# Moving six transposes of x from TensorE to DMA, cutting later loads into 3 KB runs, and starting attention work earlier in the second pass

## The chip, the cores and the metric

The kernel runs on one core of a Trainium2 chip. A core has five engines with instruction streams of their own: TensorE (PE, matrix products, with its weight loads shown apart as PEld), VectorE (DVE), ScalarE (ACT), GpSimd (POOL) and SyncE (SP), and sixteen DMA engines that move data between the memories. The time of a run is the device time of the one core in microseconds (us); lower is better. The time before the change is the median of three runs, 248.25 us (248.21 to 249.76).

## The reference

The reference computes an attention whose keys and values are mixed between blocks, and feeds its output to a gated feed-forward network. Cut to what matters:

```python
B, H, S, D = 4, 8, 768, 64              # batches, heads, tokens, head size; 8 blocks of C = 96 tokens
P = sort_net                            # (B, H, 8, 8)
for _ in range(5):                      # exp, divide by row sums, divide by column sums
    P = exp(P - P.max(-1)); P /= P.sum(-1); P /= P.sum(-2)
k_sorted = einsum('bhij,bhjcd->bhicd', P, k_blocks)    # the same for v
attn = softmax(q_block @ k_sorted_block.T / sqrt(D))   # within each block of 96 tokens
x = (attn @ v_sorted_block) -> (B * S, H * D)          # 3072 tokens x 512
g, val = x @ w_gate, x @ w_val          # 512 -> 1536
out = (g * sigmoid(g) * val) @ w_out    # 1536 -> 512, float32
```

Inputs and output are float32. The kernel multiplies in bf16 and accumulates in float32.

## The kernel before, in words

**Tiles and stages.** The feed-forward part works in eight passes, `ffn(0)` to `ffn(7)`; pass n takes 384 tokens: half of batch n // 2. A pass has 12 steps m. `gate(n, m)` and `value(n, m)` are four matmuls each, of 128 x 384, over the four chunks kc of the model dimension; ACT takes a tanh of the gate's result and two DVE operations make the product h. In between stand the output products of the pass before, `outp(n - 1, t3, part)`: three row tiles of 128 tokens, each in three parts of four matmuls of 128 x 512. ACT copies a finished tile to SBUF and SP writes it out.

**Attention.** x for a pass comes from four units of attention, unit u = half * 4 + g, and unit g of a half makes exactly chunk kc = g of the pass's x. So `gate(n, 0)` needs unit 0's (or 4's) part first and unit 3's (or 7's) part as its fourth matmul. A unit is: `scores` (8 matmuls of the stored keys against queries into a PSUM tile of two banks, tagged "a" or "b"), `exps` on ACT, `av` (8 matmuls into a tile of the same tag, then on DVE a reciprocal and a product that writes the tile `st`, from a pool of three). `st` has tokens on partitions; the feed-forward part wants them along the free dimension. Two ways lead there. `xtr` makes four PE transposes into PSUM (`x_to`, L352) and a DVE copy into the tile `xt`. `x_dma` (L367) issues one transposing DMA from SP's queue, `st` to `xt`, and PE and DVE do nothing.

**Which unit takes which way.** `units()` (L542) decides: batch 0 and the first four units of batch 1 by PE, all later ones by DMA. The first four units of batch 0 are written out by hand ahead of the passes (L497 to L528).

**Order of the work.** PE's and POOL's order is the order of the program text (a manual schedule); DVE's, ACT's and SP's order is left to the framework's scheduler after L538. `merge(main, side)` (L570) lays the side work into a pass: main items have costs in us (0.65 for a gate or value, 0.87 for a part of an output product), and a side item is put in after the first main item with which the sum of costs reaches its due time. In pass 1 the side work is: `kq_chunk` for batch 1, three times two chunks of 16 (keys mixed and queries turned, 64 matmuls in all for each due time, one chunk drained by DVE and one by ACT), `v_chunk` for batch 1 (four times 16 matmuls), and then units 0 to 3 of batch 1. Within `units`, a pair of units has its scores at `at`, the second exp at `at + 1.3`, the two `av` at `at + 1.9` and `at + 3.6`, and each PE transpose a `lag` after its `av`.

**Loads.** All loads that convert float32 to bf16 are issued by POOL, in order, and travel on the software queue q0; SP's transfers travel on the hardware queue q1. POOL issues batch 0's v, q and k, the weights, batch 1's v (L157), k and q (L159 to L161, in two pieces of 64 and 32 tokens of each block), the output weights, and then behind four copies of v, keys and values of batches 2 and 3 (`load_k_pair`, L599, L600) and the conversion of their queries into a scratch tensor in DRAM (`q_cast`, L370). A load's tile is one row of 96 x 64 elements for each partition, so that a whole row of k or v lands as one run of 12,288 bytes.

**The end.** The last row tile's output (`out_halves`, L430) is made in two halves of 256 columns; ACT drains the first, DVE the second, and SP writes each out.

## Time and profile before

| of the profiled execution | value |
|---|---|
| its own device time | 248.79 us |
| its span, from the first to the last instruction | 246.7 us |
| PE busy | 236.6 us (96% of the span) |
| PE weight loads busy | 140.3 us (57%) |
| DVE busy | 157.7 us (64%) |
| ACT busy | 109.8 us (45%) |
| POOL busy | 50.3 us (20%) |
| granted TensorE clock | 1.00 |
| bytes on q0 (POOL's loads) | 14.16 MB in 18480 packets |
| bytes on q1 (SP's transfers) | 9.84 MB in 18176 packets |

The span is shorter than the device time by 2.1 us, which lie around it. The profiled execution is 0.54 us above the median of the three runs. In the answers of the trace a line gives the start in us, the time that the instructions take together, engine, line, operation, output and inputs, shape, count, and in brackets how long the engine sat idle before it and which work ended that. A matmul's shown time is longer than its share of a stream, because matmuls overlap: the cost of one in a stream is the distance from its start to the next one's.

Pass 0 begins at about 25 us, pass 1 at 43.1 us and pass 2 at 77.0 us.

### The profile page before, as it was taken

To read this page: it belongs to the slowest core of one execution; us is meant where nothing else is said; L and a number is where in the kernel's file an instruction comes from. 1 tells how busy PE (TensorE), PEld (TensorE's weight loads), DVE (VectorE), ACT (ScalarE), POOL (GpSimd) and SP (SyncE) were. 2 spreads that over 40 slices of the span, in tenths; PEclk is the share of its full clock that TensorE was granted. 3 is DMA by queue.
4 is the path that set the end of the run, shared out by engine and by line. 5 is a ranking of instruction groups with operands and counts; after the bars stand their busy time and mean duration, and the time that the engine had idled before them with its cause. 6 is when DMAs were issued, how large, how long until landed. Compare 5 with 4: busy or idle time off the path is not lost.

```text
span 246.7 us, 6160 instructions
## 1 busy us (share of the span) xinstructions
PE 236.6 (96%) x2609; PEld 140.3 (57%) x2633; DVE 157.7 (64%) x332; ACT 109.8 (45%) x186; POOL 50.3 (20%) x44
## 2 busy tenths in 40 slices
PE   6799999998999999999999999999999999999995
PEld 6375666575555566655555655565555555555543
DVE  6786779888455685867557746755764585446700
ACT  3977653364444444354642642254245334222311
POOL 5992139990098000000000000000000000000000
PEclk9999999999999999999999999999999999999999
DMA  5989999999999195110121111112111211100122
GB/s 96 215 121 208 206 220 210 203 224 222 183 183 161 40 201 127 45 45 0 45 74 35 58 58 35 44 43 78 32 43 45 50 48 53 43 27 20 43 82 88
DMA packets 36682, 24.38 MB, mean 99 GB/s; under 512 B 27696, under 2 KB 32560, under 8 KB 36272
## 3 DMA queue, kind: packets, MB, share of 16 engines
q0 software_dynamic: 18480, 14.16, 37.6%
q1 hardware_dynamic: 18176, 9.84, 14.2%
q8 instruction: 20, 0.33, 0.5%
q14 instruction: 6, 0.05, 0.1%
HBM read 28.32 MB, written 7.86 MB: 147 GB/s over the span
## 4 chain that ended last, share of the span: by engine, by line
PE 84%; DVE 7%; issue 3%; ACT 2%; DMA 2%; DVEq 0%; POOLq 0%
PE g_ps L386 24%; PE v_ps L404 24%; PE o_ps L421 23%; PE tkq L245 3%; PE qk L308 3%; PE av_ps L335 3%; DMA v<-in_v_dram 2%; DVE st L341 2%; DVE vt L223 1%; DVE gs_sb L396 1%; PE o_ps L437 1%; DVE h L409 1%; PE idle_ps L447 1%; PE tv L276 1%; PE x_ps L352 1%
## 5 line engine op out<-in xcount | busy, mean ns | idle before, releaser
L396 DVE SCALAR_TENSOR_TENSOR gs_sb<-th_sb,g_ps 128x384 bf16<-128x384 bf16 x96 | 52.9, 551 | 46.6 <-ACT th_sb L394 43.5
L404 PE MATMUL v_ps<-xt,wv_sb 128*128 128x384 bf16 x380 | 77.3, 326 | 0.1
L386 PE MATMUL g_ps<-xt,wg_sb 128*128 128x384 bf16 x376 | 76.6, 325 | 0.2
L394 ACT ACTIVATE th_sb<-g_ps 128x384 bf16<-128x384 f32 x96 | 47.2, 491 | 57.7 <-PE g_ps L386 55.1
L421 PE MATMUL o_ps<-wo,h 128*128 128x512 bf16 x255 | 62.1, 379 | 1.3 <-issue 0.3
L409 DVE SCALAR_TENSOR_TENSOR h<-v_ps,gs_sb 128x384 bf16<-128x384 f32 x96 | 53.3, 556 | 7.1
L404 PEld LDWEIGHTS <-wv_sb 128*128 128x128 bf16 x380 | 35.4, 97 | 23.9 <-issue 1.0
L386 PEld LDWEIGHTS <-wg_sb 128*128 128x128 bf16 x376 | 35.0, 97 | 24.3 <-issue 0.6
L421 PEld LDWEIGHTS <-h 128*128 128x128 bf16 x276 | 25.8, 98 | 27.9
L426 ACT COPY o_sb<-o_ps 128x512 f32<-128x512 f32 x23 | 13.5, 586 | 45.2 <-PE o_ps L421 45.2
L124 POOL COPY vch<-v 64x1536 bf16<-64x1536 bf16 (+2 forms) x11 | 28.7, 2639 | 14.1 <-DMA v<-in_v_dram 14.0
L321 ACT ACTIVATE e_all<-qk 96x768 bf16<-96x768 f32 x30 | 22.5, 802 | 8.4 <-PE qk L308 8.4
L341 DVE TENSOR_TENSOR st<-av_ps,r_sb 96x512 bf16<-96x512 f32 x32 | 21.7, 680 | 0.2
L335 PEld LDWEIGHTS <-e_all 96*128 96x128 bf16 x256 | 11.9, 98 | 4.9 <-ACT e_all L321 0.9
L339 DVE RECIPROCAL r_sb<-av_ps 96x8 f32<-96x8 f32 x32 | 6.4, 199 | 12.3 <-PE av_ps L335 12.2
L335 PE MATMUL av_ps<-vt,e_all 96*128 96x65 bf16 x256 | 13.1, 193 | 0.1
L223 DVE CAST vt<-tv 96x1024 bf16<-96x1024 f32 (+1 forms) x9 | 9.8, 1098 | 2.6 <-PE tv L286 1.7
L225 ACT CAST vt<-tv 96x1024 bf16<-96x1024 f32 (+1 forms) x9 | 8.1, 914 | 5.5 <-PE tv L286 3.6
L447 PE MATMUL idle_ps<-warm_sb 128*128 128x512 bf16 x22 | 6.1, 381 | 0.4 <-issue 0.2
L223 DVE COPY oh_sb<-o_ps 128x256 f32<-128x256 f32 x1 | 0.4, 425 | 9.3 <-PE o_ps L437 9.3
L371 POOL DMA_DIRECT2D q_scr<-in_q_dram x2 | 5.7, 3232 | 0.0
L122 ACT COPY vch<-v 64x768 bf16<-64x768 bf16 (+1 forms) x4 | 5.5, 1387 | 0.3 <-DMA v<-in_v_dram 0.3
(80 smaller groups left out, 133.1 us busy)
## 6 DMA issues: line engine op xcount, KB each, us to landing
out_dram<-o_sb SPq DMA_DIRECT2D x23, 256.0 KB, 2.0
v<-in_v_dram POOLq DMA_DIRECT2D x4, 384.0 KB, 12.7
wg_sb<-in_moe_w_gate_dram POOLq DMA_DIRECT2D x3, 512.0 KB, 11.3
wv_sb<-in_moe_w_val_dram POOLq DMA_DIRECT2D x3, 512.0 KB, 13.1
wo<-in_moe_w_out_dram POOLq DMA_DIRECT2D x3, 512.0 KB, 15.8
kp<-in_k_dram POOLq DMA_DIRECT2D x2, 768.0 KB, 10.0
v<-in_v_dram POOLq DMA_DIRECT2D x2, 768.0 KB, 16.5
q_scr<-in_q_dram POOLq DMA_DIRECT2D x2, 768.0 KB, 25.0
```

The source lines that it names most:

```text
L124: eng.tensor_copy(dst, src.transpose([0, 2, 1]))
L223: nc.vector.tensor_copy(dst, src)
L321: nc.scalar.activation(e_all[:, n:n + 2, 0:4 * C], wide[0:C, :, 0:4 * C], AF.Exp, scale=scale)
L335: nc.tensor.matmul(o[:, two, i4, 0:D + 1], lhsT=e[:, i4 * C:i4 * C + 128], rhs=vt[:, 2 * g + two, half * 4 + i4, 0:D + 1], start=True, sto ...
L341: nc.vector.tensor_tensor(st.rearrange("p i two d -> p two i d"), o[0:C, :, :, 0:D], r_sb.to_broadcast([C, 2, 4, D]), op=ALU.mult)
L386: nc.tensor.matmul(g_ps, lhsT=wg_sb[:, kc, ts(m, 128)], rhs=xt[:, kc, :], start=(kc == 0), stop=(kc == NKC - 1))
L394: nc.scalar.activation(th_sb, g_ps, AF.Tanh, scale=0.5)
L396: nc.vector.scalar_tensor_tensor(gs_sb, th_sb, 1.0, g_ps, op0=ALU.add, op1=ALU.mult)
L404: nc.tensor.matmul(v_ps, lhsT=wv_sb[:, kc, ts(m, 128)], rhs=xt[:, kc, :], start=(kc == 0), stop=(kc == NKC - 1))
L409: nc.vector.scalar_tensor_tensor(h_tiles[n][:, m, :], v_ps, 0.5, gs_tiles.pop(m), op0=ALU.mult, op1=ALU.mult)
L421: nc.tensor.matmul(o_ps, lhsT=h_w[:, m, ts(t3, 128)], rhs=wo_sb[part][:, m % 4, :], start=(m == 0), stop=(m == NFC - 1))
L426: nc.scalar.copy(o_sb, o_ps)
```

## The change

Five things are changed.

1. `units()` sends x by DMA for all units but 2 and 3 of each half of batch 0. In practice that is units 4 and 5 of batch 0 and units 0 to 3 of batch 1: six units that went by PE before. Units 6 and 7 of batch 0 stay with PE.
2. The tiles of k, q and v get four groups of 24 tokens with a gap of 16 elements after each, and loads other than batch 0's write group by group: runs of 24 x 64 bf16 elements, 3,072 bytes. Batch 0's first tiles keep the dense layout.
3. The k and q loads of batch 1 are split 48 and 48 tokens, not 64 and 32.
4. The side work of pass 1 has new due times: key and query chunks at 0.6, 3.9 and 7.2 (before 4.6, 5.9 and 10.4), value chunks at 5.2, 5.8, 8.5 and 9.1 (before 7.2, 7.9, 8.5, 9.1), units at 10.4 and 15.1 (before 11.7 and 16.4), with the second `av` of a pair 3.2 after the scores (before 3.6).
5. The last half of the last row tile is drained in two quarters, by DVE and ACT, and written out from two queues, SP's and ACT's.

```diff
+    GC = C // 4
+    def nat_tile(pool, name, tag):
+        return pool.tile([128, 4, GC * D + 16], BF16, name=name, tag=tag)
+    def grouped(t):
+        return t[:, :, 0:GC * D].rearrange("p s (c d) -> p s c d", d=D)
+    def dense(t):
+        return t.rearrange("p s n -> p (s n)")[:, 0:C * D].rearrange("p (c d) -> p c d", d=D)
+    def load_groups(tile4, rows, src, lo, hi):
+        nc.gpsimd.dma_start(out=tile4[rows, lo:hi, 0:GC * D],
+                            in_=src[:, lo * GC:hi * GC, :].rearrange("p (s c) d -> p s (c d)", c=GC))
...
-        nc.gpsimd.dma_start(out=kq_tile(b)[rows, lo:hi, :], in_=k_nat[b, :, lo:hi, :])
+        load_groups(kq_tile(b), highr, k_nat[b], lo, hi)
...
-            nc.gpsimd.dma_start(out=kq_tiles["p"][u * R:(u + 1) * R], in_=k_nat[2 + u])
+            load_groups(kq_tile("p"), slice(u * R, (u + 1) * R), k_nat[2 + u], 0, 4)
...
+        if b == 0:
+            nc.gpsimd.dma_start(out=dense(v_tile(0))[rows, lo * GC:hi * GC], in_=v_nat[0, :, lo * GC:hi * GC, :])
+        else:
+            load_groups(v_tile(b // 2), rows, v_nat[b], lo, hi)
...
-    for lo, hi in ((0, 64), (64, C)):
+    for lo, hi in ((0, 2), (2, 4)):
         load_k(1, lo, hi)
         load_q(1, lo, hi)
...
-            drain(eng, o_sb, o_ps)
-            nc.sync.dma_start(out=out[ds(base, 128), cols], in_=o_sb)
+            if part == 0:
+                drain(eng, o_sb, o_ps)
+                nc.sync.dma_start(out=out[ds(base, 128), cols], in_=o_sb)
+                continue
+            for e, queue, lo in (("v", nc.sync, 0), ("s", nc.scalar, DM // 4)):
+                drain(e, o_sb[:, lo:lo + DM // 4], o_ps[:, lo:lo + DM // 4])
+                queue.dma_start(out=out[ds(base, 128), ds(DM // 2 + lo, DM // 4)], in_=o_sb[:, lo:lo + DM // 4])
...
-    def units(b, us, ats, lags=(3.1, 3.1)):
+    def units(b, us, ats, avs=(1.9, 3.6), lag=3.1):
...
-            for w, tag, t in ((u, "b", 1.9), (u2, "a", 3.6)):
-                if b == 0 or b == 1 and u < H2:
+            for w, tag, t in ((u, "b", avs[0]), (u2, "a", avs[1])):
+                if b == 0 and u % H2 >= 2:
                     todo.append((at + t, lambda w=w, tag=tag: av(b, w, tag)))
                     todo.append((at + t + lag, lambda w=w: drain("v", *xtr(b, w))))
                 else:
                     todo.append((at + t, lambda w=w, tag=tag: (av(b, w, tag), x_dma(b, w))))
...
-    merge(ffn(1), kqs(1, (4.6, 5.9, 10.4)) + vs(v_chunk, 16, (7.2, 7.9, 8.5, 9.1))
-          + units(1, range(4), (11.7, 16.4), (3.1, 2.4)))
+    merge(ffn(1), kqs(1, (0.6, 3.9, 7.2)) + vs(v_chunk, 16, (5.2, 5.8, 8.5, 9.1))
+          + units(1, range(4), (10.4, 15.1), (1.9, 3.2)))
```

More of the change, by code (lines that the diff above doesn't have):

```diff
@@ L84, with kq_at, v_tile @@
     v_tiles = {}
+    GC = C // 4
[8 more added lines that the diff above has]
+                            in_=src[:, lo * GC:hi * GC, :].rearrange("p (s c) d -> p s (c d)", c=GC))
     def kq_tile(b):
         if b not in kq_tiles:
-            kq_tiles[b] = natp.tile([128, C, D], BF16, name=f"kq{b}", tag="nat")
+            kq_tiles[b] = nat_tile(natp, f"kq{b}", "nat")
         return kq_tiles[b]
+    def kq_at(b, c):
+        return grouped(kq_tiles[b])[:, c // GC, c % GC, :]
     def load_k(b, lo, hi):
-        rows = highr if b else lowr
-        nc.gpsimd.dma_start(out=kq_tile(b)[rows, lo:hi, :], in_=k_nat[b, :, lo:hi, :])
+        load_groups(kq_tile(b), highr, k_nat[b], lo, hi)
     def load_k_pair():
-        kq_tiles["p"] = natp.tile([128, C, D], BF16, name="kp", tag="nat")
         for u in range(2):
-            nc.gpsimd.dma_start(out=kq_tiles["p"][u * R:(u + 1) * R], in_=k_nat[2 + u])
+            load_groups(kq_tile("p"), slice(u * R, (u + 1) * R), k_nat[2 + u], 0, 4)
     def load_q(b, lo, hi):
-        rows = lowr if b else highr
-        nc.gpsimd.dma_start(out=kq_tile(b)[rows, lo:hi, :], in_=q_nat[b, :, lo:hi, :])
-    def load_v(b, lo, hi):
-        if b // 2 not in v_tiles:
-            v_tiles[b // 2] = vnp.tile([128, C, D], BF16, name=f"v{b // 2}", tag="vn")
-        u = b % 2
-        nc.gpsimd.dma_start(out=v_tiles[b // 2][u * R:(u + 1) * R, lo:hi], in_=v_nat[b, :, lo:hi, :])
+        load_groups(kq_tile(b), lowr, q_nat[b], lo, hi)
+    def v_tile(pair):
+        if pair not in v_tiles:
+            v_tiles[pair] = nat_tile(vnp, f"v{pair}", "vn")
+        return v_tiles[pair]
+    def load_v(b, lo, hi):
+        rows = slice(b % 2 * R, (b % 2 + 1) * R)
+        if b == 0:
+            nc.gpsimd.dma_start(out=dense(v_tile(0))[rows, lo * GC:hi * GC], in_=v_nat[0, :, lo * GC:hi * GC, :])
+        else:
+            load_groups(v_tile(b // 2), rows, v_nat[b], lo, hi)
     def load_w(sb, dram, lo, hi):
@@ L119, in copy_v @@
         dst = vch3[rows, d0:d1, cs]
-        src = v_tiles[pair][rows, cs, d0:d1]
+        src = (dense(v_tiles[0])[rows, cs, d0:d1] if rows == lowr else
+               grouped(v_tiles[pair])[rows, s, :, d0:d1])
         if eng is nc.scalar:
@@ L135 @@
     halves = (lowr, highr)
-    qk0 = natp.tile([128, C, D], BF16, name="qk0", tag="nat")
+    qk0 = dense(nat_tile(natp, "qk0", "nat"))
     k0 = qk0[:, 0:HC, :]
@@ L142, in load_q0 @@
         nc.gpsimd.dma_start(out=q0[t].rearrange("p c d -> p (c d)"), in_=q_runs[0, t])
-    load_v(0, 0, HC)
-    load_v(0, HC, C)
+    load_v(0, 0, 2)
+    load_v(0, 2, 4)
     make_identity(nc, ident)
@@ L156 @@
     load_gv(1024, DF)
-    load_v(1, 0, HC)
-    load_v(1, HC, C)
-    for lo, hi in ((0, 64), (64, C)):
+    load_v(1, 0, 2)
+    load_v(1, 2, 4)
+    for lo, hi in ((0, 2), (2, 4)):
         load_k(1, lo, hi)
@@ L245, in kq_chunk @@
                 nc.tensor.matmul(tp[two * D:(two + 1) * D, lc, :],
-                                 lhsT=kq_tiles[b][:, at + lc, :],
+                                 lhsT=kq_at(b, at + lc),
                                  rhs=rm[:, two], start=True, stop=True)
@@ L356, in xtr @@
         half, g = divmod(u, H2)
-        if g == 0:
-            xts[(b, half)] = xtp.tile([128, H2, TW], BF16, name=f"xt{b}_{half}", tag="xt")
         x_ps = xt_tile("x", 1)[:, 0]
@@ L546, in units @@
             u, u2 = us[2 * n:2 * n + 2]
-            lag = lags[n]
             held = []
@@ L598 @@
     load_k_pair()
-    load_v(2, 0, C)
-    load_v(3, 0, C)
+    load_v(2, 0, 4)
+    load_v(3, 0, 4)
     q_cast(2)
```

## The prediction

> **What bounds the kernel now.** I read the page first: busy times and the rows of slices.

> ```profile
> PE 236.6 (96%) x2609; PEld 140.3 (57%) x2633; DVE 157.7 (64%) x332; ACT 109.8 (45%) x186; POOL 50.3 (20%) x44
> ...
> PE   6799999998999999999999999999999999999995
> ...
> DMA  5989999999999195110121111112111211100122
> ```

> PE is full from the fifth slice (25 us) to the end, so each microsecond of matmul that goes, and each wait of PE that goes, comes off the end. A slice is 6.17 us: the DMA row says that all sixteen DMA engines are full from 6 to 80 us and nearly idle afterwards. All six units that the change sends by DMA fall into the full part. Nothing in this trace does: the first transposing DMA is issued at 81.4 us. That is the main unknown.

> Then the timeline of PE, for what a transpose costs and where PE waits between 25 and 80 us.

> ```profile
> 73.94 0.34 PE L352 MATMUL x_ps<-ident,st 96*128 96x96 bf16 x4
> 74.11 1.89 PE L421 MATMUL o_ps<-wo,h 128*128 128x512 bf16 x7
> ```

> From start to start the four transposes take 0.17 us, not the 0.34 shown, since matmuls overlap.

> ```profile
> 56.84 0.63 PE L276 MATMUL tv<-rmix,vch 128*128 128x64 bf16 x16 [0.20 <-DVE vt L223]
> ...
> 60.17 0.44 PE L245 MATMUL tkq<-rmix,kq 128*64 128x64 bf16 x16 [0.52 <-issue]
> ...
> 68.49 0.34 PE L308 MATMUL qk<-kqt 64*128 64x96 bf16 x8 [0.35 <-DVE st L341]
> ```

> These are the waits of the second pass, measured by starts: 16 value matmuls take 0.46 (53.79 to 54.25), the third group began at 56.02 and the fourth only at 56.84: 0.36 lost. Key chunks take 1.14 (48.70 to 49.84), the last took 58.70 to 60.55: 0.71 lost. Scores take 0.45 (62.38 to 62.83), those at 67.80 took until 68.76: 0.51 lost. In the first pass a value group took 0.83 and not 0.65 (39.28 to 40.11): 0.18. Together 1.76 us.

> Last the DMA answers: landing of SP's transfers over the whole span (first two lines, the median) and from 60 to 82 us (third line).

> ```profile
> out_dram<-o_sb SPq DMA_DIRECT2D x23, 256.0 KB, 2.0
> ...
> xt<-st SPq DMA_TRANSPOSE x20, 2.4
> ```

> ```profile
> out_dram<-o_sb SPq DMA_DIRECT2D x3, 256.0 KB, 5.9
> ```

> An output write lands 2.0 us after its issue on quiet engines and 5.9 beside the load stream: 3.9 more. In the packet records, the two writes at 64.8 and 71.5 wait 3.1 us longer than a quiet one for their first packet; the other 0.8 is slower moving.

> **The change part by part.**

> *Transposes.* Six units less on PE: 6 x 0.17 = 1.0 us off PE, on the path, since PE is never free. DVE loses six copies of 0.35 us = 2.1 us. In 25 to 43 us DVE is busy 15.7 of 18.0, so this takes away the 0.18 wait there too. SP gets six issues of 1.2 us; its queue is nearly empty then (three writes from 64.8 to 78).

> *Due times of pass 1.* The key, query and value chunks are the same matmuls, spread over about 16 us (from the first gate on) rather than 12 (48.7 to 60.5), so DVE's five drains of 1.2 us are less crowded. The 0.36 is a wait for a DVE drain of the same PSUM tag; it gets two more FFN groups of distance. The 0.71 is no wait for data: PE stops in the middle of a chunk, after 48 of 64 matmuls, "issue". The packet records have an instruction page (queue q8, 16 KB) at 57.83 that took 0.94 us: PE ran out of instructions behind the load stream. Counted from the instruction at which quiet pages are fetched, pages come 3 to 4 us late beside runs of 1 to 8 KB and about 5 beside 12 KB. Fewer instructions per us and shorter runs should let this wait go. The 0.51 is the pair's second scores behind the DVE product of `av` of the unit before; the new order puts a value, a gate and a value (1.95 us) between them, not one part of an output product (0.87). Gain 1.58 of these three; against it the scores of unit 1 now follow the last value chunk's DVE drain (1.22 us) after 1.3 us, and I allow 0.3 for a new wait. If DVE were behind there, it would cost up to one drain, 1.2.

> *Are keys and values there?* The first key chunk moves from 48.7 to about 43.4. It needs the first pieces of k and q, which land at 40.0 and 42.4 in the trace and are now a quarter smaller (1.2 us earlier in all), less 0.9 us for the two transposes' packets between them: about 42, 1.4 us to spare. The second chunk needs the second pieces (44.9, with the transposes about 46) and comes near 48. The value chunks need POOL's copies, done at 48.0, and start near 50.5.

> *3 KB runs.* In the window 20.5 to 22.2 us runs of 3,072 bytes fill q0 (the second query piece of batch 0) and 211 GB/s move; from 53 to 64 us runs of 12,288 bytes and 216 GB/s. So the runs cost q0 2%, some 1 us at its end near 80, which nothing waits for. A run holds an engine 0.25 us rather than 0.91 (11 us x 16 engines over some 193 runs).
> [...]

> *x of units 4 and 5 of batch 0.* `st` is written at 32.72 and 34.86 (DVE's rows of L341). Quiet landing 2.4 gives 35.1 and 37.3, with the writes' extra 3.9 it gives 39.0 and 41.2. `gate(1, 0)` now starts at 43.11 - 0.34 - 0.18 = 42.6. In time if the extra wait w is under 5.3.

> *x of units 0 to 3 of batch 1.* This is the tight one. By the due times `av` of unit 3 stands after the tenth gate; behind it come three FFN groups (1.95) and three parts of an output product (2.61). With its own 0.25, pass 2 starts 4.8 us after this `av`, and the fourth chunk of x is wanted at 5.3. From an `av` to its finished `st` go 1.85 us (66.55 to 68.43, 71.32 to 73.20), then 2.4 + w. PE stalls for 1.85 + 2.4 + w - 5.3 = w - 1.05. Before, the PE transposes there had no wait. w is bounded by 0 (no load beside it) and 3.9 (the writes, just in this stretch, where the query conversion runs until 79). The instruction page at 73.69 came some 1.7 late, the writes' first packets 3.1. I take 2.5, between these: transposes do not write to DRAM as the writes do, but share their queue. Stall 1.45, from 0 to 2.85.

> [...] A transpose of 384 packets is 24 to an engine. [...]

> *Last drain.* A DVE copy takes 0.68 us for 512 columns and 0.425 for 256, so about 0.295 for 128: 0.13 less, ACT's quarter beside it. ACT's queue has not been used before; SP's first transfer landed 1.7 us after issue like a late one. From -0.3 to +0.5; taken -0.1.

> *Sum*: -1.0 - 1.76 + 0.3 - 0.1 + 1.45 = -1.1 us. The profiled execution, 248.79, would become 247.7. It lies 0.54 above the median of the runs; from 248.25 it gives **247.1**.

> **Rivals.**

> *A: the transposes barely wait* (w near 1). No stall at pass 2: -2.6, 245.7; with no new wait on DVE 245.3. For it: shorter runs, little data (98 KB). Against: both writes in the same stretch.

> *B: slower, by alternation.* If an engine takes one packet of the transpose and then one run of the load, each of 24 packets costs 0.25 us more: 6.0 us for a unit, and unit 5 queues behind unit 4. Unit 4 lands at 32.7 + 2.4 + 3.1 + 6.0 = 44.2, unit 5 near 47 (its later packets meet 1 KB weight runs of 0.1 us). `gate(1, 0)` waits about 4 us, and the seventh `st`, from a pool of three, waits for unit 4's transfer too and holds DVE. 248.25 - 2.55 + 4 + 1.4 = 251.1, reaching 249.5 to 253. It decides once unit 5 lands after 43.7 (42.6 plus the 1.1 won). [...]

> *C: the change doesn't do what it says:* the waits of pass 1 only move, because DVE still has its 1.2 us drains beside 1.1 us of FFN work for every 1.3 us of PE. Then 1 us is won and 1.45 lost: 248.6.

> **How the numbers follow.** Forecast 0.43, with its own range 245.7 to 248.5 by w; A 0.31; B 0.20; C 0.06. The 8-in-10 range takes in A and reaches into B: 245.2 to 250.9; left out are B's upper half and the ends. About 1% (2.5 us) is what a measurement of this kernel can tell from no change. Faster by more is most of A, 0.29; slower by more is most of B, 0.19; the rest 0.52.

> **What would show it.** No PE rows of L352's line between 34 and 39 and between 69 and 77 us. The six transposes' landings: 4 to 6 us says forecast, under 3.5 A, over 8 B. PE idle in the first gate of pass 2, released by the DMA into xt: 0.5 to 2.9 us says forecast; such a wait near 42.6 says B. The "issue" gap in a key chunk gone. I would be wrong if keys landed after 43.4, if DVE's backlog moved into the scores at about 59, or if the output writes on SP's queue held the transposes back.

## The result, and the profile after

| | before | after |
|---|---|---|
| device time, median (lowest to highest) | 248.38 us (248.21 to 249.76) | 255.19 us (254.3 to 256.8) |
| ratio, with its 95% interval | 1 | 1.0269 (1.02 to 1.0337) |
| the profiled execution: device time / span | 248.79 / 246.72 us | 254.55 / 252.46 us |
| first value group of pass 0, of pass 2; last matmul's end | 23.49, 78.19, 243.64 | 23.40, 83.71, 249.19 |

The changed kernel is 6.8 us slower by the medians and 5.8 us in the two profiled executions. The last row places the 5.8: from pass 0's first value group to pass 2's first one the kernel before takes 54.70 us and the changed one 60.31, which is 5.61 more; from there to the last matmul both take the same (165.45 and 165.48); the end is 0.19 longer. So nearly all of it happens in pass 1 and at the gate that opens pass 2.

The changed kernel's page, busy times and rows of slices (6.31 us to a slice):

```profile
PE 238.6 (95%) x2585; PEld 140.5 (56%) x2609; DVE 156.4 (62%) x326; ACT 110.2 (44%) x187; POOL 50.7 (20%) x44
...
PE   7799996799999899999999999999999999999994
...
PEclk9999999599999999999999999999999999999999
...
DMA  5999999999999169401102111111111111101122
```

PE has 24 instructions less, the six units' transposes, and is nevertheless 2.0 us longer busy. The row of PE dips in the seventh slice (38 to 44 us), and in the eighth PEclk, the clock that the throttle granted, is 5: half speed. Nothing like it stands in the page of before.

The DMA answers of the changed kernel, from issue to landing: of the transposes issued from 32 to 34 us, from 34 to 36, and from 66 to 84, and of the output writes in that last stretch.

```profile
xt<-st SPq DMA_TRANSPOSE x1, 11.4
...
xt<-st SPq DMA_TRANSPOSE x1, 12.8
...
out_dram<-o_sb SPq DMA_DIRECT2D x3, 256.0 KB, 5.4
xt<-st SPq DMA_TRANSPOSE x4, 6.5
```

Quiet transposes land in 2.3 us, and in the packet records their first packet moves 1.2 us after the issue. Unit 4's takes 11.4 (32.66 to 44.07), unit 5's 12.8 (34.79 to 47.55); the first four of batch 1 take 6.9, 6.6, 6.3 and 5.0. Then DVE and PE, in the timeline from 40 to 52 us:

```profile
44.16 0.69 DVE L365 TENSOR_TENSOR st<-av_ps,r_sb 96x512 bf16<-96x512 f32 x1 [3.21 <-DMA xt<-st]
```

```profile
41.18 0.81 PE L408 MATMUL g_ps<-xt,wg_sb 128*128 128x384 bf16 x4
45.36 1.44 PE L426 MATMUL v_ps<-xt,wv_sb 128*128 128x384 bf16 x4 [3.37 <-DVE gs_sb L418]
46.60 0.52 PE L376 MATMUL x_ps<-ident,st 96*128 96x96 bf16 x4
46.92 0.52 PE L408 MATMUL g_ps<-xt,wg_sb 128*128 128x384 bf16 x1
47.59 1.12 PE L408 MATMUL g_ps<-xt,wg_sb 128*128 128x384 bf16 x3 [0.15 <-DMA xt<-st]
48.64 1.92 PE L269 MATMUL tkq<-rmix,kq 128*64 128x64 bf16 x64
```

The releaser named for the first wait of PE is a DVE product, but it is only the messenger: DVE's own line shows that it stood 3.21 us for a transpose to land. `st` comes from a pool of three; the `st` of this line is unit 7's, the eighth, which must overwrite unit 4's, the fifth, and unit 4's transfer has not read it yet; the FFN products queued behind it on DVE then hold PE. By starts, PE loses 3.53 us ahead of the value group (the gate at 41.18 is done with its 0.65 at 41.83) and 0.35 in the gate behind it, which waits for unit 5.

The second thing is in the durations. The value group takes 1.24 us from start to start and not 0.65, the key chunk 1.85 and not 1.14. The windows give the clock (the column after the engines):

```profile
44.27:51.09 6.82, 5.58 (x78) 3.33 (x78) 4.79 (x10) 0.97 (x2) 6.82 (x7) 0.50 1.23 201
51.09:57.90 6.81, 6.81 (x118) 4.59 (x117) 4.88 (x8) 3.55 (x6) 4.54 (x2) 1.00 1.13 213
```

The clock halved while PE stood idle and stayed so for 6.83 us. From 45.36 to 51.43 PE worked off, less the 0.35 wait, what costs 3.35 us at full clock (two groups, a transpose group, a key chunk, the next value group), in 5.72: 2.4 us lost.

Last the gate of pass 2, which waits for units 2 and 3 of batch 1:

```profile
81.03 0.49 PE L408 MATMUL g_ps<-xt,wg_sb 128*128 128x384 bf16 x2
81.93 0.32 PE L408 MATMUL g_ps<-xt,wg_sb 128*128 128x384 bf16 x1 [0.41 <-DMA xt<-st]
83.01 0.32 PE L408 MATMUL g_ps<-xt,wg_sb 128*128 128x384 bf16 x1 [0.75 <-DMA xt<-st]
```

By starts 0.58 and 0.91, together 1.5 us. The account of the first value groups' distance closes, with 1.0 for the transposes taken from their rows before the change: 54.70 - 1.0 (transposes) - 1.1 (due times, measured below) + 3.5 + 0.35 + 2.4 + 1.5 = 60.35, against 60.31.

### The profile page after: what moved, and what is told of

It is laid out like the page before. It is cut to its first block, busy times and chain, and to the rows that moved or that the text cites. A ratio compares the mean times of both kernels' runs of the same rounds, so it can differ in the third digit from the quotient of the medians.

```text
span 252.5 us, 6126 instructions
## 1 busy us (share of the span) xinstructions
PE 238.6 (95%) x2585; PEld 140.5 (56%) x2609; DVE 156.4 (62%) x326; ACT 110.2 (44%) x187; POOL 50.7 (20%) x44
## 4 chain that ended last, share of the span: by engine, by line
PE 77%; DMA 9%; DVE 7%; issue 3%; ACT 2%; DVEq 0%; POOLq 0%
PE o_ps L443 22%; PE g_ps L408 21%; PE v_ps L426 21%; DMA xt<-st 7%; PE tkq L269 3%; PE qk L332 2%; PE av_ps L359 2%; DMA v<-in_v_dram 2%; DVE gs_sb L418 2%; DVE st L365 2%; DVE vt L247 1%; PE o_ps L459 1%; ACT th_sb L416 1%; PE idle_ps L474 1%; PE tv L300 1%
## 5 line engine op out<-in xcount | busy, mean ns | idle before, releaser
L426 PE MATMUL v_ps<-xt,wv_sb 128*128 128x384 bf16 x380 | 78.2, 329 | 4.0 <-DVE gs_sb L418 3.8
L408 PE MATMUL g_ps<-xt,wg_sb 128*128 128x384 bf16 x376 | 77.6, 328 | 1.4 <-DMA xt<-st 1.3
L408 PEld LDWEIGHTS <-wg_sb 128*128 128x128 bf16 x376 | 35.1, 98 | 25.1 <-issue 1.7
## 6 DMA issues: line engine op xcount, KB each, us to landing
out_dram<-o_sb SPq DMA_DIRECT2D x23, 256.0 KB, 2.0
```

The lines of the kernel that those rows point to most:

```text
L408: nc.tensor.matmul(g_ps, lhsT=wg_sb[:, kc, ts(m, 128)], rhs=xt[:, kc, :], start=(kc == 0), stop=(kc == NKC - 1))
L426: nc.tensor.matmul(v_ps, lhsT=wv_sb[:, kc, ts(m, 128)], rhs=xt[:, kc, :], start=(kc == 0), stop=(kc == NKC - 1))
```

## The experiments

The first two questions were what a transpose waits for, and whether the late x, the pool or the clock holds the end. All times are device times; the kernel before, run beside them, had medians of 248.4 to 248.5.

| kernel | what it is | us, median (range) | ratio to before, 95% |
|---|---|---|---|
| e1 | after, loads in runs of 6 and 12 KB | 254.67 (253.86 to 255.48) | 1.0241 (1.0197 to 1.0284) |
| e2 | after, loads in runs of 1 KB | 252.71 (251.05 to 253.98) | 1.0163 (1.0112 to 1.0215) |
| e3 | after, units 4 and 5 on PE | 250.72 (250.66 to 251.65) | 1.0099 (1.0062 to 1.0135) |
| e4 | after, all six on PE | 248.41 (248.25 to 248.57) | 0.9994 (0.9981 to 1.0007) |
| e5 | after, idle matmuls in the wait | 256.76 (254.71 to 257.27) | 1.0317 (1.028 to 1.0354) |
| e6 | after, six `st` buffers | 254.87 (254.51 to 255.3) | 1.0257 (1.0235 to 1.0279) |
| e7 | before, split last drain only | 248.83 (248.52 to 250.61) | 1.003 (1.0011 to 1.005) |
| e8 | 3 KB runs and due times only | 247.76 (247.56 to 248.04) | 0.9975 (0.9964 to 0.9985) |
| e9 | e8 with units 4 and 5 by DMA | 254.77 (254.28 to 255.5) | 1.0244 (1.0216 to 1.0272) |
| e10 | due times only (runs of 6 and 12 KB) | 247.71 (247.59 to 249.46) | 0.9973 (0.9957 to 0.9989) |
| e11 | e8, second value chunk drained by ACT | **247.14** (246.9 to 247.25) | 0.9941 (0.9923 to 0.996) |
| e12 | e8, value chunks further apart | 250.17 (249.29 to 251.27) | 1.0066 (1.004 to 1.0092) |

e3's row holds three of its four runs, those with a clock of 0.999 to 1.0; the fourth, the profiled one, ran at 0.986 and took 254.82.

### Run length: e1 and e2

e1 removes the gaps between the groups, so that neighbouring groups join into one run; e2 cuts the tiles into twelve groups of eight tokens.

```diff
-        return pool.tile([128, 4, GC * D + 16], BF16, name=name, tag=tag)
+        return pool.tile([128, 4, GC * D], BF16, name=name, tag=tag)
```

```diff
-    GC = C // 4
+    GC = C // 12
...
-        return pool.tile([128, 4, GC * D + 16], BF16, name=name, tag=tag)
+        return pool.tile([128, 12, GC * D + 16], BF16, name=name, tag=tag)
...
+        lo, hi = 3 * lo, 3 * hi
```

> The changed kernel, but the gap between the groups of a tile is gone, so that a piece of 48 tokens lands in one run of 6,144 bytes and a whole row in one of 12,288. Theory of turns (an engine takes one packet of the transpose, then one run of the load): while unit 4's transpose is in flight beside runs of 6 KB, its packets go at the rate of the runs, about 33 per us and not the 62 per us seen beside 3 KB; unit 4 lands near 46 and unit 5 near 49 us (44.1 and 47.6 in the changed kernel; both catch up when the 1 KB weight runs begin near 44), and the time grows by 1 to 3 us. Rival, a wait that does not depend on the runs (the transposes are slow by themselves beside any load): landings and time as in the changed kernel, within 0.5 us.

> The changed kernel with runs of 1,024 bytes (groups of 8 tokens) in place of 3,072. Theory of turns: each of the 24 packets per engine waits 0.1 us and not 0.25, so unit 4 lands near 40 and unit 5 near 42 us, the waits of PE and DVE between 40 and 48 us go, the TensorE clock stays at 1.00, and the time falls to what the forecast gave, 246.5 to 248.5. If instead many small descriptors cost the loads their rate, keys land late and the time stays over 250. Rival, a wait that does not depend on the runs: unit 4 at 44, unit 5 at 47.5 and 254 to 256 us as before.

The landings of units 4 and 5: 40.94 and 43.59 with 1 KB, 44.07 and 47.55 with 3 KB, 46.51 and 49.27 with 6 KB. The DMA answers for 38 to 41 us, a stretch that lies inside unit 4's and 5's transfers in all three, give packets by queue (packets, MB, share of 16 engines). First 1 KB, then 3 KB, then 6 KB:

```profile
q0 software_dynamic: 357, 0.35, 85.9%
q1 hardware_dynamic: 352, 0.08, 46.8%
```

```profile
q0 software_dynamic: 167, 0.45, 95.8%
q1 hardware_dynamic: 163, 0.04, 10.4%
```

```profile
q0 software_dynamic: 108, 0.53, 92.5%
q1 hardware_dynamic: 112, 0.03, 6.9%
```

One packet of the transposes moves for each packet of the load (some 20 of q0's are 4 bytes long), at all three lengths. A unit's 384 packets therefore take some 384 runs of the load at each of these lengths: at 163 packets in 3 us that is 7.1 us, and from unit 4's first packet at 36.5 to its landing it is 7.6. A second part of the lateness does not follow the run length: the first packet comes 3.8 us after the issue at 3 KB, 3.9 at 1 KB and 4.1 at 6 KB, 2.7 to 2.9 more than a quiet one's.

The times did not follow as expected. In e1 PE's first wait grew to 5.6 us, and yet the kernel is no slower (254.67 against 255.19, with ranges that overlap): pass 2's gate has no wait left, where it lost 1.5 us in the changed kernel.

```profile
83.07 0.81 PE L408 MATMUL g_ps<-xt,wg_sb 128*128 128x384 bf16 x4
```

In e2 the waits of pass 1 nearly went (0.39 and 0.42 us, clock 1.0 in the profiled run) and pass 2's gate took over:

```profile
76.85 0.32 PE L412 MATMUL g_ps<-xt,wg_sb 128*128 128x384 bf16 x1 [0.60 <-DMA xt<-st]
79.56 0.32 PE L412 MATMUL g_ps<-xt,wg_sb 128*128 128x384 bf16 x1 [2.40 <-DMA xt<-st]
```

That gate now comes 5.3 us earlier (75.75 against 81.03), in a part of the load stream where unit 3 of batch 1 lands 6.8 us after its issue and not 5.0. The profiled run is e2's fastest, 251.05; the other three have clocks of 0.986 to 0.992.

### Which of the six units costs: e3, e4 and e9

Each changes the condition in `units()` that sends a unit by PE: e3 puts units 4 and 5 of batch 0 back on PE, e4 all six, e9 batch 1's four.

```diff
-                if b == 0 and u % H2 >= 2:
+                if b == 0:
```

```diff
-                if b == 0 and u % H2 >= 2:
+                if b == 0 or b == 1 and u < H2:
```

```diff
-                if b == 0 and u % H2 >= 2:
+                if b == 0 and u % H2 >= 2 or b == 1 and u < H2:
```

`xtr` allocates the tile `xt` where it handles a half's first unit. e9 has the last half drained whole as well, as in e8; e3 and e4 keep the split drain.

> The changed kernel, but units 4 and 5 of batch 0 go by PE again; units 0 to 3 of batch 1 stay with DMA. If the loss comes from units 4 and 5 (DVE held by the pool of st, gate of pass 1 waiting, half clock afterwards), it goes: 247 to 248.5 us, with a wait of about 1.5 us left at the first gate of pass 2. If the four units of batch 1 or the new due times cost the time, it stays over 252.

> The changed kernel, but all six units go by PE as before the change; 3 KB runs, new due times and the split last drain stay. By the prediction's terms the due times are worth 1.76 less 0.3, the drain 0.1: 246.5 to 247.5 us, and the 'issue' gap in a key chunk is gone. Rival: the due times only move the waits, 248 us within 0.5.

> The changed kernel with x of batch 1's first four units back on PE and the last half drained whole: only units 4 and 5 of batch 0 go by DMA. Theory (the loss is made where pass 1 waits for these two units): unit 4 lands near 44, unit 5 near 47.5, PE waits 3.4 us in pass 1's first value group and 0.5 us at the next gate, the clock halves from about 44 to 51, and pass 2 starts 5.7 us later than with these two units on PE (83.7 less the 1.5 of waits there, plus 0.67 for four PE transposes, against 77.1), with no wait at its gates. 247.8 + 5.7 = 253.5, from 252.8 to 254.0. Rival (two costs that simply add: batch 1's four units cost 2.8 us when they went by DMA alone, so these two cost the rest, 6.8 - 2.8 = 4.0): 251.8.

e4 brings the time back to that of before, so the transposes by DMA are the whole loss; it lies at its rival's 248, not at the 246.5 to 247.5 expected, because the split last drain, which it keeps, takes back what the due times win (e7 and e8 below). e3 lies between its two expectations. Each part alone is a loss too, and they do not add: units 4 and 5 alone cost 254.77 - 247.76 = 7.0 us (e9 against e8), batch 1's four alone 250.72 - 248.41 = 2.3 (e3 against e4), both together 255.19 - 248.41 = 6.8. The two waits and the clock row of e9:

```profile
PEclk9999999779999999999999999999999999999999
```

```profile
45.87 0.81 PE L428 MATMUL v_ps<-xt,wv_sb 128*128 128x384 bf16 x4 [3.59 <-DVE gs_sb L420]
...
48.16 1.12 PE L410 MATMUL g_ps<-xt,wg_sb 128*128 128x384 bf16 x3 [1.15 <-DMA xt<-st]
```

By starts 3.75 and 1.16 us, and some 2.6 of half clock, which is what the waits leave of the 7.2 by which pass 2's first value group is later than in e8. It was 1.3 us above what the theory asked for, partly because unit 5 landed at 48.12 here, and far above the 251.8 of the rival that adds the two costs.

In e3's profiled run the gate of pass 2 waits 0.49 and 3.17 us by starts:

```profile
77.10 0.32 PE L410 MATMUL g_ps<-xt,wg_sb 128*128 128x384 bf16 x1 [0.32 <-DMA xt<-st]
80.43 0.48 PE L410 MATMUL g_ps<-xt,wg_sb 128*128 128x384 bf16 x1 [3.01 <-DMA xt<-st]
```

Four transposes less on PE (0.7 us) against 3.66 of waits is 3.0. In this run the clock halved as well, from 79.57 to 86.40; the other three, with a clock of 1.0, lie 2.2 to 3.2 us above e4's median. The profiles fit this reason for the two losses not adding: the first delays pass 2's gate past the worst of the load stream (unit 3 of batch 1 lands 7.2 us after its issue in e3 and 5.0 in the changed kernel), and so takes over part of the second wait.

### The pool and the clock: e6 and e5

e6 gives `st` six buffers; e5 adds, behind the last gate of pass 0, 16 matmuls of 512 columns on constant data into a tile that nothing reads.

```diff
-        st = ssp.tile([C, 4, 2, D], BF16, name="st", tag="st")
+        st = ssp.tile([C, 4, 2, D], BF16, name="st", tag="st", bufs=6)
```

```diff
+                if (n, m) == (0, NFC - 1):
+                    todo.append((0.0, lambda: fill(pair_tile("keep_ps", "b")[:, 0:512], 16)))
```

> The changed kernel with six buffers for st in place of three. Theory: DVE is no longer held by unit 4's transfer; units 6 and 7 go on, and PE waits instead at the first gate of pass 1, for unit 4 (44 us) and unit 5 (47.5 us). Since unit 5's landing ends both, the time stays within 1.5 us of the changed kernel's 254.3 to 256.8. Rival, the pool of three is the real cause: the time falls under 251.

> The changed kernel with sixteen idle matmuls of 128 x 512 (3.5 us, results unused) behind the last gate of pass 0, where PE stands idle from 41.8 to 45.4 us. Theory: the idle time itself is set by the landing of unit 4's transpose, but it also halves the granted TensorE clock from 44.3 to 51.1 us; with PE kept busy the clock stays at 1.00, the first key chunk takes 1.14 us and not 1.85, and the time falls by 1.0 to 2.5 us though PE does more. Rival, the half clock comes from something else, such as the load stream, and costs little: the clock drops as before and the time stays or grows by up to 1 us.

With six buffers DVE does not stand, and PE waits at pass 1's first gate for the transposes themselves. The timeline of e6:

```profile
45.03 0.34 PE L408 MATMUL g_ps<-xt,wg_sb 128*128 128x384 bf16 x1 [1.81 <-DMA xt<-st]
48.39 1.12 PE L408 MATMUL g_ps<-xt,wg_sb 128*128 128x384 bf16 x3 [3.02 <-DMA xt<-st]
```

The time is the same: the pool only chooses where PE waits.

In e5 the idle matmuls keep the clock at 1.0 through pass 1. The key chunk takes 1.14 us again, and pass 2's gate comes at 79.71 and not 81.03 (its third and fourth matmul wait there, 1.04 and 2.43 us), but unit 3 of batch 1 lands at 83.62 all the same. PE's first wait and the last one in the timeline of e5:

```profile
45.80 0.81 PE L426 MATMUL v_ps<-xt,wv_sb 128*128 128x384 bf16 x4 [0.32 <-DVE gs_sb L418]
...
83.66 0.48 PE L408 MATMUL g_ps<-xt,wg_sb 128*128 128x384 bf16 x1 [2.27 <-DMA xt<-st]
```

What pass 1 won, pass 2's gate took, and in that longer wait the clock halved instead (83.57 to 86.98). From pass 0's to pass 2's first value group e5 takes 61.40 us, 1.1 more than the changed kernel. The expected gain of 1 to 2.5 us was missed; what e5 shows is that the slow key chunk came from the clock and that the clock's loss is covered by the next late transpose. One of its runs, the only one with a clock of 0.999, took 254.71, the other three, at 0.993, 256.7 to 257.3.

### The two parts left: e7, e8, e10, and two tries to gain more

e7 is the kernel before with the last half drained by DVE and ACT. e8 is the changed kernel with `b == 0 or b == 1 and u < H2` and the whole drain, so the 3 KB runs and the due times remain; e10 is e8 without the gaps. e11 and e12 change e8's value chunks: e11 the engine that drains the second (s is ACT, v is DVE), e12 the due times.

```diff
-        return [(at, lambda m=m: f(1, m * size, size, "sv"[m % 2], "ba"[m % 2])) for m, at in enumerate(ats)]
+        return [(at, lambda m=m: f(1, m * size, size, "sssv"[m], "ba"[m % 2])) for m, at in enumerate(ats)]
```

```diff
-    merge(ffn(1), kqs(1, (0.6, 3.9, 7.2)) + vs(v_chunk, 16, (5.2, 5.8, 8.5, 9.1))
+    merge(ffn(1), kqs(1, (0.6, 3.9, 7.2)) + vs(v_chunk, 16, (5.2, 6.5, 8.5, 9.8))
```

> The kernel before with only the last drain split in two quarters, on DVE and ACT and on two queues. The prediction's term: 0.1 us faster. Rival from the traces of the runs so far: ACT's quarter starts only when DVE's is done (ACT waits for the DVE copy of the same tile), the last landing comes 0.1 later after the last matmul, and the end's waits 0 to 0.45 us later, so 0.1 to 0.6 us slower.

> All six units by PE and the last drain whole as before the change; of the change only the 3 KB runs and the due times of pass 1 are left. By the marks of the run with all six units on PE, which started pass 2 1.06 us earlier than the kernel before and kept that to its last matmul: 247.2 to 247.5 us, 0.9 to 1.1 us faster than the kernel before. Rival: the due times' gain is lost at the end for another reason than the drain, and the time is 248.2 to 248.5.

> All six units on PE, whole last drain, the new due times, but no gaps between the groups: k, q and v land in runs of 6,144 bytes (batch 1's 48-token pieces) and 12,288 bytes (whole rows). Theory that the due times alone made the gain (an instruction page is then late at a place with nothing to lose): 247.8 as with 3 KB runs, within 0.2. Rival (the short runs matter, because pages come later behind 12 KB runs): the 0.7 us stop in a key chunk, released by issue, is back and the time is 248.2 to 248.5.

> All six units on PE, 3 KB runs, new due times, whole last drain; and the drain of the second value chunk goes from DVE to ACT (the fourth stays on DVE). Theory: PE's wait of 0.64 us at the gate-and-value pair near 54 us is DVE's backlog of the key chunk's drain and this one, so it goes, and the time is 247.1 to 247.3. Rival (ACT's own queue becomes late and the wait moves to the next chunk of the same tag or to the scores): 247.6 to 248.0.

> All six units on PE, 3 KB runs, whole last drain, new due times but value chunks at 5.2, 6.5, 8.5 and 9.8 in place of 5.2, 5.8, 8.5 and 9.1. Theory: one more FFN group between the drains gives DVE 0.65 us, the wait of 0.64 us near 54 us goes or halves, 247.1 to 247.5. Rival (DVE is short of time over the whole stretch, so the wait only moves to the later chunk): 247.6 to 248.0.

The split drain costs 0.4 us by e7's median and 0.65 by e4 against e8, which differ in it alone. The changed kernel's last lines show one reason:

```profile
249.23 0.29 DVE L247 COPY oh_sb<-o_ps 128x128 f32<-128x128 f32 x1 [9.33 <-PE o_ps L459]
...
249.55 0.27 ACT L249 COPY oh_sb<-o_ps 128x128 f32<-128x128 f32 x1 [1.26 <-DVE oh_sb L247]
```

The two quarters are two writes to one tile, and ACT starts only when DVE's copy is done: one after the other they take 0.59 us, longer than DVE's whole half did (0.42 us in the profile of before). ACT's own transfer lands 0.27 us after SP's. From the last matmul's end to the span's end it is 3.1 us in before and e8 and 3.3, 3.6 and 3.65 in the changed kernel, e7 and e4; what makes the difference between these three stays open. That two tiles in place of one would let the engines work side by side was not tried.

The due times gain: from pass 0's to pass 2's first value group 53.59 us in e8 and in e10, against 54.70, and 0.6 us in the median, where e8's expectation held 0.9 to 1.1. Run length makes no difference (247.76 and 247.71), and neither e8 nor e10 has a stop of PE released by "issue" in pass 1. That stop is not of one size in the old order: 0.71 us in the profile of before, 1.54 by starts in e7's:

```profile
61.07 0.44 PE L245 MATMUL tkq<-rmix,kq 128*64 128x64 bf16 x16 [1.35 <-issue]
```

One wait of PE is left in e8's pass 1, 0.64 us by starts:

```profile
54.91 0.81 PE L428 MATMUL v_ps<-xt,wv_sb 128*128 128x384 bf16 x4 [0.47 <-DVE gs_sb L420]
```

The FFN product on DVE stands behind the drain of a value chunk:

```profile
53.17 1.22 DVE L247 CAST vt<-tv 96x1024 bf16<-96x1024 f32 x1 [0.33 <-PE tv L300]
```

The expectation of e11 counted the key chunk's drain in as well, but DVE was idle for 0.33 us between the two. Giving the second value chunk to ACT (e11) removes it; no wait of PE is shown between 43 and 82 us then, and 247.14 us is the best time of all, 0.6% under before. Spreading the chunks (e12) moved the fourth one directly ahead of the scores of batch 1's first pair, whose second scores need its drain, and the wait grew, to a time that neither theory nor rival had:

```profile
62.27 0.35 PE L332 MATMUL qk<-kqt 64*128 64x96 bf16 x8 [1.82 <-DVE vt L247]
```

e12's eight runs fall in two groups: four at a clock of 1.0, 249.29 to 249.50, and four at 0.993, 250.84 to 251.27. The medians of the two groups differ by 1.6 us, and the profiled run, one of the slower group, shows the clock at half for 3.41 us behind the wait. The other group was not profiled.

## Why the prediction was wrong, point by point

**The failed step is "x of units 4 and 5 of batch 0".** It took the output writes' extra wait, 3.9 us, for the transposes and found them in time if w was under 5.3, so the sum holds nothing for them. The runs show w of 9.0 and 10.4, and PE lost 3.9 us in waits for the two and 2.4 to the half clock behind them. In unit 4's 9.0 the longer wait for the first packet is 2.7, near the 3.1 that the writes had shown; the other 6.4 are slower moving, which the writes' figure put at 0.8. That figure came from 60 to 82 us, where q0 carries mostly small packets: before has 12,400 under 512 bytes among its 12,887 packets there, and in the changed kernel the 12,461 of q0 from 66 to 84 us hold 1.96 MB, 157 bytes each. Beside runs of 3 KB, turn by turn, each packet of SP's waits for some 20 times the bytes. In the packet records of before, the last 2 KB packets of the output write at 71.5 start 0.11 us apart beside the load, those of a quiet write 0.09, which would fit one small packet slipped in between each two. The prediction did not weigh enough that such a price grows with the other queue's run: from 38 to 41 us 352 packets of SP's moved beside runs of 1 KB, 163 beside 3 KB and 112 beside 6 KB.

**Rival B held, at less than half of the price.** Its landings, 44.2 and near 47, were measured as 44.07 and 47.55; its wait of 4 as 3.9; the `st` that holds DVE (the eighth, not the seventh) is the line shown above. It said 251.1. In the profiled execution's own terms (251.6) it was 2.9 us short: 2.4 are the half clock, which no theory had; 0.4 are the due times that won 1.1 and not 1.5; 0.3 the end, taken as a gain of 0.1 and measured as a loss of 0.2. The other runs of the changed kernel lie up to 2.3 us above the profiled one, and no profile says why.

**The transposes (-1.0)** agree with the account above, which closes to 0.1 us, but no run measured them alone.

**Due times.** Forecast -1.58 with a new wait of 0.3. The new wait exists, at a gate and value and not at the scores, and is 0.64; the whole is -1.1 in the traces and -0.6 in the medians. The rest may lie in the forecast's own offset: it took a stop of 0.71, read from one execution, off the median, though the stop is 0.71 in one profile and 1.54 in another; no run near the median was profiled. Shorter runs are not what removed the stop: e10 has runs of 6 and 12 KB and no stop. The other reason of the prediction, the new order of instructions, is what is left; which part of that order it was, and whether a late instruction page made the stop, no run shows.

**Keys and values in time:** first pieces landed at 40.3 and 42.2, the second at 44.3 and 46.1, as forecast (42 and 46).

**3 KB runs** cost the loads little: e8's last query conversion landed at 79.57, before 78.97; less than the 1 us forecast.

**x of units 0 to 3 of batch 1.** The formula, stall = w - 1.05, held in four kernels. With w of unit 3 from its issue and landing (less 2.4): after 2.6, so 1.55, measured 1.49; e2 4.4, so 3.4, measured 3.33; e3 4.8, so 3.7, measured 3.66; e5 4.6, so 3.5, measured 3.47. The w taken, 2.5, was right only because pass 1 had become late and pass 2's gate came at 81.03; where it came at 75.75 to 79.71 (e2, e3, e5) w is 4.4 to 4.8, beyond the 3.9 that the prediction held for the upper end. Beside small packets the wait for the first packet is most of w: in the changed kernel unit 0's comes 5.1 us after its issue, 3.9 more than quiet in a w of 4.5, behind an output write whose own took 4.0; the 768 packets of units 0 and 1 then move in 2.5 us beside packets of 128 bytes.

**Last drain** (-0.1, from -0.3 to +0.5): +0.4. That ACT's quarter would wait for DVE's was not seen.

**Rivals A and C.** A fell with the landings: none of the six took less than 5.0 us. C fell with e8: the waits of pass 1 do not only move, and the due times win 0.6 us.

## What to carry to other kernels

In these traces a transfer of many small packets that shares the DMA engines with a load goes one packet for one run of the load: price it as its packets on each engine times the other queue's run (here 24 times 0.25 us, 6.0, where unit 4 measured 6.4), add the longer wait for its first packet (2.7 to 2.9 us more than quiet here at every run length, 3.9 behind an output write of the same queue), and do not price it by a transfer measured beside another run length. Where PE has no slack, as here, a transpose of 0.17 us on PE was worth more than a free one that landed 5 to 13 us later. After a wait is found, look at the granted clock behind it and at the next late transfer: the one added 2.4 us to waits of 3.9 here, the other took back what e2 and e5 had won.

## What the runs showed of the hardware that was not expected

| window, us | idle in it, us | clock behind it |
|---|---|---|
| e12 60.06 to 63.47 | 1.82 | 0.5 |
| after 40.85 to 44.27 | 2.27 | 0.5 |
| e9 44.05 to 47.46 | 2.27 | 0.5 |
| e3 76.16 to 79.57 | 2.47 | 0.5 |
| e5 80.15 to 83.57 | 3.04 | 0.5 |
| e6 44.60 to 48.01 | 3.08 | 0.5 |
| e1 43.01 to 46.43 | 3.41 | 0.5 |
| e9 40.63 to 44.05 | 1.77 | 1.0 |
| e2 74.68 to 78.09, then to 81.51 | 1.58, 1.47 | 1.0 |
| e6 41.18 to 44.60 | 1.44 | 1.0 |

e2's waits of 0.60 and 2.40 us fell across a boundary and cost no clock in that run. e12's two groups of runs would fit this, if where its wait of 1.82 us falls in the grid is a matter of chance; only one of its runs was profiled. A single gap of 1.82 us was enough in e12's profiled run. The half clock lasted a second window where its first one held 0.71 us or more of idle time (e1 1.38, after 1.25, e3 0.86, e9 0.71), and ended with the first where that held 0.38 or less (e6 0.38, e5 0.10, e12 under 0.05). So the time at half clock was 6.83 us in four of these seven cases and 3.41 in three.

**The runs of e12 with the lower clock took 1.6 us more**: the medians of its two groups, at clocks of 0.993 and 1.0, differ by that, and the profiled run of the first group had 3.41 us at half clock. That would be one reason why kernels with waits of about 2 us, such as e2, have a wide spread of times.
